# Sliding-window attention times a gated block on one core: seven block products in all four token chunks, and the weight work laid out anew

## The chip, the cores and the metric

One core of a Trainium2 chip runs the kernel. Its engines work beside each other, each in the order of its own instruction stream: TensorE (PE, matmuls; PEld loads the stationary operand), VectorE (DVE), ScalarE (ACT), GpSimd (POOL) and SyncE (SP, which here issues every DMA). The metric is the device time of one execution in microseconds.

## The reference, cut to what matters

```python
x = A_x                                   # (1, 2048, 576) float32
xn = layernorm(x)
q, k, v = split(xn @ wqkv)                # 32 heads of 18
p = softmax(mask(q @ k.T * 18 ** -0.5))   # causal, a window of 256 keys
s = (p @ v) @ wo
h = (xn @ w_gate) * (xn @ w_up)           # 4608 features, no nonlinearity
g = silu(h @ w_down)
out = x + s * g
```

All inputs are float32. The kernel reaches that accuracy with 16-bit floats by splitting each operand into a high and a low half and adding three products (high x high, high x low, low x high). The gate and up products and the down product are most of the matmul work.

## The kernel before, in words

A first stretch normalises x into `XT` (features on partitions, 2048 tokens along the row, high and low halves), makes v, then q and k, and stores them to DRAM. It is over about 179 us into the profiled execution. Then the main part runs in 72 slots: 18 groups of 256 features (`g`), and in each group four chunks of 512 tokens (`c`). A slot has 16 places. At each place the program writes out a few gate and up matmuls (`seven_place`, L1075, or in the main loop, L1216) and then everything that `at(slot, place, f, ...)` has put there, with the score matmuls first, then the down products, then the rest in the order in which it was registered. Place numbers beyond 15 run on into the next slots. This list alone sets the order of each engine's stream; the engines then wait for each other where data or buffers ask for it. Four kinds of work share the slots:

- **Gate and up.** In chunks 0, 1 and 2 (`SEVEN`), the product of the group's weights (two blocks of features) and the chunk (two halves of tokens), each also cut in two along the contraction, is made from seven block products in place of eight. They need sums of blocks of the input (`SX`, `XD` and parts of `XT` overwritten, made once by `s_steps`, whose places and engines are in `SUMS_AT` and `SUMS_ON`) and sums of blocks of the weights (`TF` and, split into halves, `TW`, made for each group by `t_sum` on POOL, `t_hi` on ACT, `t_lo` on DVE). A slot has 100 such matmuls of 256 columns. Products are added up in PSUM or by reading a bank (`seven_read`): product 0 is copied by ACT (L1043), and product 1 is then added on in the same bank; five others go through DVE (L1047); four multiplications of gate by up follow, three on POOL and one on DVE (L1053). In chunk 3 the slot has 52 full matmuls of 512 columns and four half ones, one ACT copy (L924) and one DVE multiplication (L929) for each of two feature tiles.
- **Down.** `down` (eight times a slot, at places 7 to 21 of the next slot, six matmuls each, L952) multiplies the result by the group's down weight into a single bank `dn`, and DVE adds each to the accumulator (L957) before the next can start. `h_hi` (L934, ACT) and `h_lo` (L939, DVE) split the input of it.
- **Attention.** Step `s` stands in slot `s + 1`: loads of k, q and v, scores (L826), maximum on DVE (L834), exponent on ACT (L840, L844, L847), the low half of the probabilities (`turn_probs`, L855, on POOL or DVE), a transposing DMA (L858), the product with v (`weigh`, L867), `finish` and, every fourth step, stores (`store_o`).
- **The next group's weights.** `ffn_raw` loads them (each gate and up load in two pieces of two DMAs, L147 and L149; the down weight, L373), `ffn_amax` takes maxima (L380, DVE), `ffn_spread_out` and `ffn_spread_in` send them through DRAM to all partitions, `ffn_scale` makes scales (L400, then L127 to L131), `up_hi`, `dn_hi` and `t_hi` are ACT's high halves (L152), `up_lo`, `dn_lo` and `t_lo` DVE's low halves (L155), and `dn_low` a scaled copy on POOL (L525). For group `g` they are placed relative to slot 4g - 4, most of them in places 38 to 68.

At the end the output weight is prepared the same way (`wo_*`), and `o_out` makes 16 output tiles (L1178, L1181).

Of the kernel before, what the change touches and what calls it, by code (L numbers as in the profile page):

```python
# [20 lines left out]
def kernel(  # L21
# [71 lines left out]
    def up_ring():  # L93
        return ring.tile([128, 10, 128], F16, name="upw", bufs=8)
# [174 lines left out]
    def square(dst, src):  # L269
        nc.scalar.activation(junk[0:src.shape[0], 0:src.shape[-1]], src, AF.Square, accum_out=dst)  # L270
# [41 lines left out]
    def qk_split(m):  # L312
        if m < QM:
            w = UW["q", m] = up_ring() if m < 8 else pro.tile([128, 10, 128], F16, name="wq8")
# [67 lines left out]

    def ffn_spread_out(g):
# [34 lines left out]
    SEVEN = (0, 1, 2)  # L418
    TF, TW, SX, XD = {}, {}, {}, {}

    def seven(sl):
        return sl % NCH in SEVEN

    def t_sum(g, kind, pair, i):
        r = RAW[g, kind].rearrange("p k (f n) -> p k f n", f=2)
        b = {(k, f): r[:, 2 * k:2 * k + 2, f] for k in range(2) for f in range(2)}
        if i == 0:
            TF[g, kind, pair] = sums.tile([128, 2, 2, 128], F32, name="tf", bufs=2)
        t = TF[g, kind, pair]
        if pair == 0:  # L430
            x0, x1 = (b[0, 1], b[0, 0]) if i == 0 else (b[1, 1], t[:, 0])
        else:
            x0, x1 = (b[1, 0], TF[g, kind, 0][:, 1]) if i == 0 else (b[1, 1], b[0, 1])
        nc.gpsimd.tensor_tensor(t[:, i], x0, x1, op=OP.subtract)

    def t_hi(g, kind, pair):
        if pair == 0:
            TW[g, kind] = sums.tile([128, 4, 2, 2, 128], F16, name="tw", bufs=2)
        w = TW[g, kind][:, 2 * pair:2 * pair + 2, 0]
        hi(w, TF[g, kind, pair], SC[g][:, 6 + kind:7 + kind])  # L440

    def t_lo(g, kind, pair):
        w = TW[g, kind][:, 2 * pair:2 * pair + 2]
        lo(w[:, :, 1], TF[g, kind, pair], SC[g][:, 6 + kind:7 + kind], w[:, :, 0])
# [5 lines left out]
    def s_steps(c):  # L450
# [13 lines left out]
        def do(e, to, x, y, f):  # L464
            if to in ("w", "z") and to not in t:
                t[to] = sums.tile([128, 2, 2, 128], F32, name="tf", bufs=2).rearrange("p a b n -> p a (b n)")
# [86 lines left out]
    SUMS_AT = ((-24, -24, -24, -23, -22, -22, -22, -17, -16, -16, -15, -15, -14, -13, -12, -11, -11),  # L553
               (-22, -22, -22, -20, -19, -18, -18, -18, -17, -17, -14, -14, -13, -12, -12, -12, -7),
               (-10, -10, -9, -8, -6, -5, -4, 3, 4, 5, 6, 7, 8, 9, 10, 11, 13))
    SUMS_ON = ("vvvvppvpvvpppvvvp", "ppppvpvpvvppvpvpv", "ppvvvpvpvvvpvpvpv")
    for c in SEVEN:
# [5 lines left out]
    for n in range(4):  # L563
        at(0, (-9, -9, -7, -7)[n], t_sum, 0, 0, n // 2, n % 2)
        at(0, (-3, -2, -1, -1)[n], t_sum, 0, 1, n // 2, n % 2)
    for n in range(4):
        at(0, (-4, -4, 0, 0)[n], t_hi, 0, n // 2, n % 2)
        at(0, (-3, -2, 1, 1)[n], t_lo, 0, n // 2, n % 2)
# [120 lines left out]
    for t in range(16):  # L689
# [35 lines left out]
        for m in range(QM):  # L725
            for c in (2 * half, 2 * half + 1):
# [4 lines left out]
                if half == 1:  # L731
                    if m in (1, 2, 3):
                        ffn_amax(0, m - 1, c - 2)
                    if m >= QM - 2:
                        k = 2 * (m - QM + 2) + c - 2
                        up_hi(0, k)
                        up_lo(0, k)
# [29 lines left out]
            else:  # L767
                if m == 3:
                    ffn_spread_out(0)
                if m == 5:  # L770
                    ffn_spread_in(0)
                if m == 6:
                    ffn_scale(0)
# [76 lines left out]
    PL_AT = ((), (0, 1, 2, 3))  # L850

# [407 lines left out]
```

## Time and profile before

| | |
|---|---|
| time, median of 3 runs | 1617.65 us (1616.84 to 1618.41) |
| the profiled execution | 1621.29 us, its span 1619.6 us |
| clock granted to PE, mean | 0.999 |
| PE busy | 1586.2 us, 98% of the span |
| DVE busy | 1307.6 us, 81% |
| ACT busy | 1115.0 us, 69% |
| POOL busy | 818.3 us, 51% |
| instructions | 39383 |

The profile is that of one execution. Times of single rows count from the start of its span. A row of the timeline has start, length, engine, line, operation, output and inputs, shapes and a count; in brackets stands the idle time of the engine before it and what ended it. A row of the windows view gives for one stretch the busy time of each engine with its number of instructions, the granted clock, the share of the DMA engines' time and the rate. A row of the groups gives the shapes and the count, then busy us and the mean ns of one, then the idle time before them. A row of the waits gives the total us, how often, and the longest.

### The profile page before, as it was taken

The numbers are of one execution on the slowest core, as the hardware profiler recorded it, in microseconds if no ns is written. First come the engines' busy times: TensorE is split into PE (matmuls) and PEld (weight loads), VectorE is DVE, ScalarE is ACT, GpSimd is POOL, SyncE is SP. The second block draws the span as 40 slices with busy tenths as digits, with TensorE's granted clock in tenths as the row PEclk, the third lists the DMA queues.
The fourth block names the chain that finished last, engine by engine and source line by source line (L and its number), as shares of the span: only waits on it lengthen the run. The fifth ranks groups of instructions, "written<-read, shape, count | busy, mean of one in ns | idle before, by whom it ended". The sixth has DMA issues, their size and how long they took to land.

```text
span 1619.6 us, 39383 instructions
## 1 busy us (share of the span) xinstructions
PE 1586.2 (98%) x14706; PEld 1164.2 (72%) x14706; DVE 1307.6 (81%) x3120; ACT 1115.0 (69%) x2180; POOL 818.3 (51%) x1050
## 2 busy tenths in 40 slices
PE   8999899999999999999999999999999999999999
PEld 5464577786868676768686777777786868686777
DVE  7536788888887989798989888888988898977644
ACT  6433487778787878787878778887878787843230
POOL 3114464556455656566665657465656565633100
PEclk9999999999999999999999999999999999999999
DMA  9572446565758786978787887878677879760158
GB/s 231 176 187 87 129 76 128 87 129 95 127 103 132 132 135 126 136 135 131 132 138 138 128 146 112 155 113 150 118 149 118 155 115 154 121 129 1 23 115 217
DMA packets 548768, 206.83 MB, mean 128 GB/s; under 512 B 489376, under 2 KB 529376, under 8 KB 548576
## 3 DMA queue, kind: packets, MB, share of 16 engines
q1 hardware_dynamic: 548576, 204.31, 67.5%
q8 instruction: 115, 1.88, 0.5%
q14 instruction: 77, 0.63, 0.1%
HBM read 76.63 MB, written 23.75 MB: 62 GB/s over the span
## 4 chain that ended last, share of the span: by engine, by line
PE 79%; DVE 12%; DMA 5%; issue 2%; POOL 1%; ACT 1%; SPq 0%; DVEq 0%; POOLq 0%; ACTq 0%
PE up L1075 27%; PE dn L952 21%; PE up L1216 10%; PE pv L867 3%; PE s L342 3%; DVE acc L957 2%; PE s L826 2%; DVE upw L155 2%; PE s L952 2%; PE s L1178 2%; PE up L1178 1%; DMA sd_f<-both 1%; PE up L342 1%; DVE gt L1047 1%; DVE ht L1053 1%
## 5 line engine op out<-in xcount | busy, mean ns | idle before, releaser
L952 PE MATMUL dn<-dnw,hh 128*128 128x288 f16 x3168 | 477.5, 286 | 14.4 <-DVE acc L957 13.2
L952 PEld LDWEIGHTS <-hh 128*128 128x128 f16 x3456 | 328.6, 98 | 150.7 <-issue 55.3
L957 DVE SCALAR_TENSOR_TENSOR acc<-dn,sc,acc 128x288 f32<-128x288 f32 x496 | 254.6, 513 | 136.0 <-PE dn L952 130.4
L840 ACT ACTIVATE mx<-mx,sig 128x1 f32<-128x1 f32 x512 | 195.3, 384 | 182.0 <-DVE mx L834 173.3
L1075 PEld LDWEIGHTS <-upw 128*128 128x128 f16 x2592 | 242.1, 97 | 33.1 <-issue 1.3
L1075 PEld LDWEIGHTS <-tw 128*128 128x128 f16 x2592 | 238.8, 97 | 32.9 <-issue 3.6
L1075 PE MATMUL up<-XT,upw 128*128 128x256 f16 x1728 | 253.9, 272 | 0.7 <-ACT gt L1043 0.7
L1216 PE MATMUL up<-XT,upw 128*128 128x512 f16 x936 | 232.0, 378 | 0.0
L1047 DVE SCALAR_TENSOR_TENSOR gt<-up,gt 128x512 f32<-128x512 f32 x270 | 184.7, 684 | 20.0 <-PE up L1075 16.5
L1053 POOL TENSOR_TENSOR ht<-gt 128x256 f32<-128x256 f32 x162 | 125.5, 788 | 125.8 <-ACT gt L1043 111.6
L1075 PE MATMUL up<-sx,tw 128*128 128x256 f16 x1296 | 175.6, 273 | 4.0 <-ACT gt L1043 2.2
L1075 PE MATMUL up<-XT,tw 128*128 128x256 f16 x1296 | 168.1, 273 | 0.0
L867 PEld LDWEIGHTS <-pt 128*128 128x128 f16 x2880 | 137.6, 96 | 29.0 <-DMA pt<-pp 1.8
L867 PE MATMUL pv<-vt,pt 128*128 128x37 f16 x2880 | 143.0, 179 | 0.6 <-DMA pt<-pp 0.6
L1216 PEld LDWEIGHTS <-upw 128*128 128x128 f16 x936 | 82.9, 97 | 68.9
L934 ACT ACTIVATE hh<-ht 128x512 f16<-128x512 f32 x144 | 89.6, 622 | 55.0 <-POOL ht L1053 34.3
L886 POOL CAST ob<-o 128x144 f16<-128x144 f32 x64 | 19.5, 304 | 202.0 <-DVE o L882 202.0
L939 DVE SCALAR_TENSOR_TENSOR hh<-hh,ht 128x512 f16<-128x512 f16 x144 | 110.6, 768 | 0.0
L1043 ACT ACTIVATE gt<-up 128x512 f32<-128x512 f32 x108 | 63.5, 588 | 59.3 <-PE up L1075 58.2
L1075 PE MATMUL up<-sx,upw 128*128 128x256 f16 x648 | 88.2, 273 | 2.4 <-DVE gt L1047 2.4
L380 DVE TENSOR_REDUCE am<-raw 128x1 f32<-128x640 f32 (+1 forms) x108 | 84.0, 790 | 0.0
L155 DVE SCALAR_TENSOR_TENSOR upw<-raw,sc,upw 128x640 f16<-128x640 f32 x72 | 76.7, 1065 | 0.3 <-ACT upw L152 0.3
(2289 smaller groups left out, 2967.4 us busy)
## 6 DMA issues: line engine op xcount, KB each, us to landing
raw<-in_B_w_down_dram SPq DMA_DIRECT2D x36, 288.0 KB
qk_d<-qp SPq DMA_DIRECT2D x18, 512.0 KB
raw<-in_B_w_gate_dram SPq DMA_DIRECT2D x36, 256.0 KB
raw<-in_B_w_up_dram SPq DMA_DIRECT2D x36, 256.0 KB
vt<-v_d SPq DMA_DIRECT2D x48, 111.0 KB
ks<-qk_d SPq DMA_DIRECT2D x96, 54.0 KB
v_d<-vo SPq DMA_DIRECT2D x16, 296.0 KB
xr<-in_A_x_dram SPq DMA_DIRECT2D x16, 288.0 KB
```

The source lines that it names most:

```text
L155: nc.vector.scalar_tensor_tensor(w, rv, s, h, op0=OP.mult, op1=OP.subtract)
L380: nc.vector.tensor_reduce(SC[g, "am"][:, half, kind:kind + 1], r, axis=AX.X if kind == 2 else AX.XY, op=OP.max, apply_absolute_value=True)
L840: nc.scalar.activation(mx[:, 1:2], mx[:, 0:1], AF.Identity, bias=sig[:, 2:3], scale=sig[:, 1:2])
L867: nc.tensor.matmul(PVB[s][:, j, i, :VW], pt[:, 2 * nb * j + n], VT[s][:, lo_ + n % nb, j * VW:(j + 1) * VW], start=n == 0, stop=n == 2 * n ...
L934: nc.scalar.activation(hh[:, 0], h, AF.Copy, scale=1.0 / LO)
L939: nc.vector.scalar_tensor_tensor(hh[:, 1], hh[:, 0], -LO, h, op0=OP.mult, op1=OP.add)
L952: nc.tensor.matmul(ps[:, :HALF], a, b, start=q == 0, stop=q == len(l) - 1)
L957: nc.vector.scalar_tensor_tensor(d, ps[:, :HALF], SC[g][:, 9:10], d, op0=OP.mult, op1=OP.add)
L1047: nc.vector.scalar_tensor_tensor(seven_new(sl, name), CH[q], H_SC, x, op0=OP.mult, op1=OP.add)
L1053: eng.tensor_tensor(HT[sl, f][:, 256 * i:256 * i + 256], u[:, 0:256], u[:, 256:512], op=OP.mult)
L1075: nc.tensor.matmul(CH[q][:, o], a, b, start=CH["first"], stop=last and q != 4, skip_group_check=q in ON)
L1216: nc.tensor.matmul(banks[up], a, b, start=i == 0 and not up, stop=i == 12 and up == 1)
```

## The change

All four chunks use the seven products; the code of the full products is gone. Around that:

- `s_steps` runs for chunk 3 too, and the places and engines of all sums are new, nearly all of them ahead of slot 0. Scratch for some of them is cut from the tile `rqk`.
- Group 0's weights are split ahead of slot 0; its bound comes from sums of squares on ACT (`first_bound`) for gate and up.
- For the other groups every piece of the weight work has a new place, from place 6 of the group before's first slot to place 5 of its own first slot. Block sums live in four tiles of two blocks (`TW[g, kind, pair]`); one sum of each kind is made twice, so POOL makes ten for each group, and not eight.
- The ring of split gate and up weights has six buffers, not eight.
- All low halves of the probabilities are made on POOL.
- The attention output tile holds two steps, not four, and is stored twice as often; the output weight's steps move; the last part writes its result in place of the accumulator and has no `yt`.

```diff
     def up_ring():
-        return ring.tile([128, 10, 128], F16, name="upw", bufs=8)
+        return ring.tile([128, 10, 128], F16, name="upw", bufs=6)
...
+    def first_bound(kind):
...
+            square(am[:, 0, kind:kind + 1], RAW[0, kind].rearrange("p k n -> p (k n)"),
+                   rv.rearrange("p k n -> p (k n)").bitcast(BF))
...
-    SEVEN = (0, 1, 2)
...
+    def t_sum(g, kind, n):
...
+        T0, T1, T3, T2 = (2, 1, 0, 3) if g == 0 else (0, 1, 0, 1)
+        to, x0, x1 = ((T0, b[0, 1], b[0, 0]), (T1, b[1, 1], t[:, T0]), (T3, b[1, 1], b[0, 1]),
+                      (T2, b[1, 0], t[:, T1]), (T0, b[0, 1], b[0, 0]))[n]
+        nc.gpsimd.tensor_tensor(t[:, to], x0, x1, op=OP.subtract)
...
-            TW[g, kind] = sums.tile([128, 4, 2, 2, 128], F16, name="tw", bufs=2)
...
+        w = TW[g, kind, pair] = sums.tile([128, 2, 2, 2, 128], F16, name="tw", bufs=4)
...
-    for c in SEVEN:
+    SUMS_AT = ((-26, -26, -26, -25, -24, -24, -23, -23, -22, -22, -21, -21, -20, -20, -20, -19, -18),
+               (-26, -26, -25, -25, -24, -24, -23, -22, -22, -21, -20, -20, -20, -20, -19, -19, -18),
+               (-17, -17, -16, -16, -15, -15, -14, -12, -11, -10, -9, -9, -8, -7, -6, -5, -1),
+               (-12, -11, -11, -10, -9, -8, -8, -7, -6, -6, -5, -4, -3, -3, -2, -1, 1))
+    SUMS_ON = ("v" * 17, "p" * 17, "v" * 7 + "p" * 10, "p" * 17)
+    for c in range(NCH):
...
+    for k in range(4):
+        at(0, -7 + k, up_hi, 0, k)
+        at(0, -6 + k, up_lo, 0, k)
...
-        (nc.gpsimd if j or i in PL_AT[seven(s + 1)] else nc.vector).tensor_tensor(pp[:, a + n:a + 2 * n], sm, pp[:, a:a + n], op=OP.subtract)
+        nc.gpsimd.tensor_tensor(pp[:, a + n:a + 2 * n], sm, pp[:, a:a + n], op=OP.subtract)
...
-                    at(b, ((0, 1, 2, 6, 10, 14) if g == 1 else (-6, -2, 2, 6, 10, 14))[2 * kind + part],
-                       ffn_raw, g, kind, part)
-                for half in range(2):
-                    at(b, ((9, 13) if g == 1 else (9, 9), (14, 26), (24, 29))[kind][half], ffn_amax, g, kind, half)
-            at(b, 30, ffn_spread_out, g)
-            at(b, 34, ffn_spread_in, g)
-            at(b, 40, ffn_scale, g)
-            for k, (ph, pl) in enumerate(((43, 45), (44, 47), (49, 53), (55, 57))):
...
-                at(b, (38, 39, 42, 44)[n], t_sum, g, 0, n // 2, n % 2)
-                at(b, (50, 51, 54, 55)[n], t_sum, g, 1, n // 2, n % 2)
...
-                at(b, (47, 47, 52, 57)[n], t_hi, g, n // 2, n % 2)
-                at(b, (48, 49, 56, 58)[n], t_lo, g, n // 2, n % 2)
-        for k, (ph, pw, pl) in enumerate(((57, 62, 64), (64, 68, 65)) if g else ((64, 65, 66), (68, 69, 70))):
...
+            at(b, (45, 47)[k] if g else 64 + k, dn_hi, g, k)
+            at(b, (46, 49)[k] if g else 65 + k, dn_lo, g, k)
+            at(b, (49, 51)[k] if g else 66 + k, dn_low, g, k)
...
+                at(b, (6, 9, 12, 15, 18, 21)[2 * kind + part], ffn_raw, g, kind, part)
+            for half in range(2):
+                at(b, (14, 16, 20, 22, 25, 27)[2 * kind + half], ffn_amax, g, kind, half)
+        at(b, 28, ffn_spread_out, g)
+        at(b, 32, ffn_spread_in, g)
+        at(b, 38, ffn_scale, g)
+        for k in range(4):
+            at(b, (40, 42, 62, 64)[k], up_hi, g, k)
+            at(b, (41, 44, 63, 65)[k], up_lo, g, k)
+        for kind in range(2):
+            for n in range(5):
+                at(b, ((40, 41, 43, 60, 61), (44, 46, 48, 61, 62))[kind][n], t_sum, g, kind, n)
+            for pair in range(2):
+                at(b, ((57, 58), (64, 66))[pair][kind], t_hi, g, kind, pair)
+                at(b, ((58, 59), (67, 69))[pair][kind], t_lo, g, kind, pair)
...
-        at(NSLOT - 4, 2 * k, wo_raw, k)
-        at(NSLOT - 4, 2 * k + 6, wo_amax, k)
-        at(NSLOT - 2, 3 * k, wo_split, k)
-    at(NSLOT - 3, 0, wo_out)
-    at(NSLOT - 3, 6, wo_in)
-    at(NSLOT - 3, 9, wo_scale)
+        at(NSLOT - 4, 2 * k + 6, wo_raw, k)
+        at(NSLOT - 4, 2 * k + 14, wo_amax, k)
+        at(NSLOT - 2, 3 * k + 2, wo_split, k)
+    at(NSLOT - 3, 8, wo_out)
+    at(NSLOT - 3, 12, wo_in)
+    at(NSLOT - 2, 0, wo_scale)
```

More of the change, by code (lines that the diff above doesn't have):

```diff
@@ new lines @@
+        if g == 0:
+            continue
+        for kind in range(3):
+            for part in range(2):
+                at(b, (6, 9, 12, 15, 18, 21)[2 * kind + part], ffn_raw, g, kind, part)
+            for half in range(2):
+                at(b, (14, 16, 20, 22, 25, 27)[2 * kind + half], ffn_amax, g, kind, half)
[5 more added lines that the diff above has]
+            at(b, (41, 44, 63, 65)[k], up_lo, g, k)
@@ L998, in seven_unit @@
         for kind in range(2):
[L999 removed]
+            w1, w2 = UW[g, kind], UW.get((g, 2 + kind))
             w, k = {0: (w1, 0), 1: (w1, 2), 6: (w2, 2)}.get(q, (None, 0))
[L1001 to L1002 removed]
+            if w is not None:
+                wh, wl = w[:, k:k + 2], w[:, 5 + k:7 + k]
+            else:
+                pair, n = {2: (0, 1), 3: (0, 0), 4: (1, 0), 5: (1, 1)}[q]
+                wh, wl = (TW[g, kind, pair][:, n, i] for i in range(2))
             if q in (2, 4, 6):
```

191 lines of the change are left out of this document (79 added, 112 removed).

## The prediction

> **What bounds the kernel now.** I read the page first, then the busy time slot by slot, then the waits at the places that the change touches.
>
> ```profile
> PE 1586.2 (98%) x14706; PEld 1164.2 (72%) x14706; DVE 1307.6 (81%) x3120; ACT 1115.0 (69%) x2180; POOL 818.3 (51%) x1050
> ```
> ```profile
> core 0: us, PE busy (x) PEld busy (x) DVE busy (x) ACT busy (x) POOL busy (x), PEclk, DMA share, GB/s
> 712.88:731.75 18.87, 18.87 (x206) 15.54 (x204) 17.25 (x42) 14.28 (x29) 12.16 (x14) 1.00 0.93 174
> 731.75:750.62 18.87, 18.87 (x206) 15.54 (x204) 15.35 (x41) 14.08 (x29) 10.08 (x14) 1.00 0.76 132
> 750.62:769.52 18.90, 18.90 (x206) 15.56 (x204) 15.26 (x42) 15.53 (x31) 12.73 (x20) 1.00 0.95 128
> 769.52:790.24 20.72, 20.01 (x163) 11.23 (x160) 20.25 (x45) 19.12 (x37) 11.77 (x14) 1.00 0.63 105
> 178.89:196.82 17.93, 13.16 (x103) 9.82 (x101) 14.14 (x21) 6.37 (x11) 14.43 (x15) 0.90 0.43 120
> ```
>
> The first four windows are one group: chunks 0, 1, 2 with seven products, chunk 3 with full ones. In the first three PE never rests; they are as short as their matmuls allow. The chunk 3 slot is 1.83 us longer, and there DVE is busy 20.25 of 20.72 us. So the kernel is bound by PE, except in chunk 3, where the weight work crowds DVE and ACT. The last window, slot 0, I use below.
>
> Small slacks keep PE busy in a seven-product slot. The down products (L952) share one bank, so each waits until DVE's addition (L957) has emptied it:
>
> ```profile
> 733.22 0.90 PE L952 MATMUL dn<-dnw,hh 128*128 128x288 f16 x6
> ...
> 754.28 0.27 PE L1075 MATMUL up<-XT,upw 128*128 128x256 f16 x1
> ...
> 760.93 0.90 PE L952 MATMUL dn<-dnw,hh 128*128 128x288 f16 x6
> ...
> 768.79 0.90 PE L952 MATMUL dn<-dnw,hh 128*128 128x288 f16 x6
> ...
> 774.89 0.90 PE L952 MATMUL dn<-dnw,hh 128*128 128x288 f16 x6 [0.71 <-DVE acc L957]
> ```
>
> The last row shows the wait when DVE is late. The row at 754.28 is the first matmul of product 1, which overwrites the bank that ACT must first copy (L1043).
>
> **The change, part by part.**
>
> *Products in chunk 3.* 18 slots go from 20.7 to 18.87 us: 18 x 1.83 = 32.9 us less, matmul time and DVE wait together. The order of PE's instructions bears it out: 44 matmuls more in each of 18 slots. DVE gains five additions and one product there and loses two multiplications and four of the probabilities' subtractions, which go to POOL; all this is what the other three slots bear already.
>
> *Raw weights and their maxima, chunk 0.* The gate weight's second piece is issued at place 9, behind the four loads of q, and its maximum stands on DVE at place 14. Before, a down weight piece was issued just there (place 10), and another maximum stood at place 14:
>
> ```profile
> 724.03 0.41 SPq L147 DMA_DIRECT2D raw<-in_B_w_up_dram  x1
> 724.49 0.54 SPq L149 DMA_DIRECT2D raw<-in_B_w_up_dram  x1
> ...
> 727.18 2.32 SPq L806 DMA_DIRECT2D qs<-qk_d  x4
> 729.54 0.42 SPq L373 DMA_DIRECT2D raw<-in_B_w_down_dram  x1
> ...
> 885.94 0.42 SPq L373 DMA_DIRECT2D raw<-in_B_w_down_dram  x1
> ```
> ```profile
> 730.64 0.81 DVE L380 TENSOR_REDUCE am<-raw 128x1 f32<-128x640 f32 x1
> 731.37 0.68 DVE L1047 SCALAR_TENSOR_TENSOR gt<-up,gt 128x512 f32<-128x512 f32 x1
> 731.97 0.51 DVE L957 SCALAR_TENSOR_TENSOR acc<-dn,sc,acc 128x288 f32<-128x288 f32 x1
> ```
> ```profile
> 602.03 3.42 DMA tf<-sd_f
> ```
>
> SP reaches the place at 729.54 (16.66 us into the slot; in the slot that begins at 867.57, 18.37 in). A piece is two DMAs, so the second goes out at 730.0. The nearest landing I have is the 192 KB read, 3.42 us after its issue: 733.4. DVE is there at 730.64 and waits 2.8 us. Behind it in the queue are 0.73 us of maximum, the 0.60 of L1047 and L957's 0.51: done at 735.2, where PE's next down product was due at 733.22. PE loses 2.0 us, or 3.7 where SP is as late as at 885.94; nothing if the landing took 1.4 us. I take 2.3, in 15 groups (those whose loads meet attention's): **+34.5**. The other pieces go out five to eight places ahead of their maxima and, by the same lag of SP, land about when DVE comes: 0.
>
> *The scale, chunk 2.* It moves from place 8 to place 6, ahead of the addition that frees the bank for 760.93:
>
> ```profile
> 760.26 0.52 DVE L957 SCALAR_TENSOR_TENSOR acc<-dn,sc,acc 128x288 f32<-128x288 f32 x1 [0.82 <-PE dn L952]
> ...
> 761.76 0.69 DVE L400 TENSOR_REDUCE sc<-tf 128x3 f32<-128x384 f32 x1
> ...
> 763.18 0.51 DVE L957 SCALAR_TENSOR_TENSOR acc<-dn,sc,acc 128x288 f32<-128x288 f32 x1
> ```
>
> The five instructions take 1.42 us (761.76 to 763.18). The gap before 760.26 holds 0.82, so the addition ends at 761.3, 0.4 after PE wants it. The two DMAs before the scale are issued two places earlier as well, so their lateness stays. 0 to 1.3; I take 0.5 x 16 = **+8**.
>
> *From chunk 2 to 3, and from 3 to 0.* At a slot's end ACT has no gap between the scores and the copy of product 0:
>
> ```profile
> 747.65 0.86 ACT L840 ACTIVATE mx<-mx,sig 128x1 f32<-128x1 f32 x2 [1.81 <-DVE mx L834]
> ...
> 752.89 0.58 ACT L1043 ACTIVATE gt<-up 128x512 f32<-128x512 f32 x1
> ...
> 764.19 0.51 ACT L847 CAST pp<-sm__12089 128x384 f16<-128x384 f32 x1
> 764.61 1.55 ACT L152 ACTIVATE upw<-raw,sc 128x640 f16<-128x640 f32 x2
> ...
> 783.13 0.71 ACT L152 ACTIVATE tw<-tf,sc 128x512 f16<-128x512 f32 x1
> 783.74 0.76 ACT L152 ACTIVATE dnw<-raw,sc 128x576 f16<-128x576 f32 x1
> ```
>
> From 747.65 on it works through to 753.47, and PE needs the copy at 754.28: slack 0.81. The change puts two down-weight casts (2 x 0.67, overlap taken off) into this run in chunk 2, so the copy is 0.53 late; the low half of an up weight (1.07, row below) now stands at place 12, ahead of the addition for 768.79, which had 0.77 to spare, in the same stretch. Together 0.5 to 1.3, taken as 0.6 x 16 = **+9.6**.
>
> At the end of chunk 3 the run gets two up-weight casts and one of the sums: 2 x 0.75 + 0.63 = 2.1, so 1.3 late. There is more: the sums' casts at places 9 and 10 stand before and behind a pair of probabilities that in chunk 2 ended at 764.70, so the second is done about 765.9. DVE's low half waits for it, and behind that are the reductions that end attention's step and the next scores:
>
> ```profile
> 765.11 0.20 DVE L878 RECIPROCAL rc<-pv 128x8 f32<-128x8 f32 x1
> ...
> 767.51 0.51 DVE L957 SCALAR_TENSOR_TENSOR acc<-dn,sc,acc 128x288 f32<-128x288 f32 x1
> 768.41 1.48 DVE L155 SCALAR_TENSOR_TENSOR upw<-raw,sc,upw 128x640 f16<-128x640 f32 x1
> ```
> ```profile
> L155 DVE SCALAR_TENSOR_TENSOR upw<-raw,sc,upw 128x640 f16<-128x640 f32 x72 | 76.7, 1065 | 0.3 <-ACT upw L152 0.3
> ```
>
> They start at 766.6 in the place of 765.11. The addition that ended at 768.02 ends near 769.5, 0.7 after PE wants it, and ACT's run starts later too. So 1.3 to 2.7; I take 1.8 x 16 = **+28.8**. The row at 768.41 shows what POOL's sums next to DVE add: 1.48 us for one low half of an up weight, against a mean of 1.07. The Trainium skill ("SBUF — State Buffer", section "SBUF: two separate sides") says that DVE reading two SBUF inputs and POOL reading SBUF exclude each other for a whole instruction; the row agrees, and the rule speaks for the upper end of these terms.
>
> *POOL in chunk 3.* The 10.1 us of chunk 1, five of the ten block sums (eight before) and the two 1/2048 copies:
>
> ```profile
> L525 POOL TENSOR_SCALAR dnw<-dnw 128x576 f16<-128x576 f16 x36 | 67.8, 1882 | 7.9 <-ACT dnw L152 7.9
> L434 POOL TENSOR_TENSOR tf<-raw,tf 128x256 f32<-128x256 f32 x72 | 59.7, 829 | 11.3 <-ACT qp L333 8.3
> ```
>
> 10.1 + 5 x 0.83 + 2 x 1.88 = 18.0 of 18.87. The copies stand before a subtraction whose transposed result is needed seven places later; 0 here, since PE's late start above covers it, else up to 1 us a group.
>
> *Before slot 0, the end, the rest.* Group 0's splits and most sums move ahead of slot 0.
>
> ```profile
> PE up L1075 <- DVE gt L1047: 3.0, 3, 1.7
> PE up L1075 <- ACT gt L1043: 2.9, 2, 2.2
> ```
>
> These sum to 5.9; the longest of the first row (1.7) is the wait for the output weight's scale near the end, the other 4.2 lie in slot 0. I take **-4**; the 17 added steps of chunk 3 could give back as much before slot 0. The output weight's maximum and its scale come one place closer: **+1**. Half-size output tiles mean 32 more DMAs on SP, hidden by its waits for probabilities; six weight buffers suffice, since two are free when the next pair is written and the other two are read last at place 13. Results written in place: nothing.
>
> *Sum.* -32.9 + 34.5 + 8 + 9.6 + 28.8 - 4 + 1 = +45. The profiled execution took 1621.29 us (span 1619.6), 3.6 over the median: 1666 there, 1663 as a median.
>
> **Rivals.** *Faster: the seven-product slot keeps its shape.* If DVE's wait for the gate piece and ACT's late copy don't occur, only the first and last terms stand: 1617.65 - 32.9 - 3 = 1582. For it speaks the load: a group's DVE work, 68.1 us in the four windows, is 90% of 4 x 18.87, and the chunk 0 window has 91% without a wait. Against it: the waits come from order, not load. It decides at (32.9 + 3)/16 = 2.2 us of waits a group; above that the kernel is slower.
>
> *Slower still: the clock.* After waits in slot 0 the clock fell:
>
> ```profile
> 189.17 2.20 PE L1075 MATMUL up<-sx,tw 128*128 128x256 f16 x12 [2.21 <-ACT gt L1043]
> ...
> 752.97 1.47 PE L1075 MATMUL up<-sx,tw 128*128 128x256 f16 x12
> ```
>
> The same twelve matmuls took 2.20 after an idle 2.21 us, and the window has a clock of 0.90. A whole slot like it is 13.16 us busy for 10.7 of work (98 matmuls at the second row's step, (1.47 - 0.27)/11 = 0.109): 2.5 us. Once a group in 15 groups this gives 1663 + 37 = 1700. The Trainium skill ("TensorE: Matmul & The Clock Gate", Part 1) lets the clock fall only after an idle window of about 3.4 us; by that rule waits of 2 to 3 us leave it whole and 1663 stands. The row differs from the rule, so the case keeps a chance.
>
> **How the numbers follow.** Forecast 0.58 (own range 1636 to 1690: its 81 us of waits a third smaller or larger); slower still 0.14; faster 0.25; no change 0.03. A measurement tells about 0.2% (3 us) from nothing. The faster cases spread from 1582 to 1614, and I leave out about half; at the top I take in the clock case and the upper ends of the waits: 1592 to 1712. Slower 0.72, same 0.03, faster 0.25.
>
> **What would show it.** Chunk 0 slots near 21 us with DVE's maximum waiting for a raw weight's DMA over 2 us; product 1 of chunks 3 and 0 waiting for ACT's copy; the down product after the scale waiting for DVE; a group of about 80.6 us against the 77.4 of the four windows. I am wrong if groups last 76 us, or if the DMA lands before DVE comes; and the size is off if PE's clock falls below 1.00 in chunk 0.

## The result, and the profile after

The changed kernel took 1771.42 us (median of 4 runs, 1766.80 to 1777.38), the kernel before, on the same chip, 1618.01 us (1616.84 to 1618.41). The ratio is 1.095, interval 1.0915 to 1.0988: slower. Its profiled execution took 1768.96 us, the span is 1767.2 us against 1619.6, and the mean clock granted to PE 0.984 against 0.999.

The first line of the page of the changed kernel answers to the first line of the prediction:

```profile
PE 1609.7 (91%) x15498; PEld 1248.3 (71%) x15498; DVE 1354.2 (77%) x3131; ACT 1118.1 (63%) x2190; POOL 979.8 (55%) x1214
```

PE is busy 23.5 us longer, but its share falls from 98% to 91%: most of the 147.6 us is PE at rest. The windows view of the changed kernel shows where: the stretch before slot 0, then slots 44 to 47, one group, chunk by chunk.

```profile
core 0: us, PE busy (x) PEld busy (x) DVE busy (x) ACT busy (x) POOL busy (x), PEclk, DMA share, GB/s
98.40:198.01 99.61, 86.37 (x478) 46.91 (x476) 58.38 (x86) 35.94 (x70) 50.01 (x50) 0.91 0.35 102
1118.01:1138.70 20.69, 19.21 (x206) 15.47 (x204) 17.32 (x40) 16.66 (x33) 15.21 (x18) 1.00 0.76 132
1138.70:1162.30 23.60, 20.80 (x206) 16.31 (x204) 17.94 (x44) 13.65 (x28) 9.39 (x13) 0.93 0.66 141
1162.30:1185.97 23.67, 20.75 (x206) 16.06 (x204) 17.04 (x44) 17.02 (x34) 14.87 (x21) 0.93 0.66 106
1185.97:1205.86 19.89, 19.19 (x206) 15.53 (x204) 16.77 (x41) 15.04 (x31) 16.02 (x18) 1.00 0.51 91
```

The first row's stretch in the kernel before:

```profile
98.40:178.89 80.49, 80.49 (x479) 45.24 (x477) 45.65 (x75) 28.94 (x56) 28.77 (x32) 1.00 0.42 126
```

So slot 0 begins 19.1 us later: PE rests for 13.2 us of the longer stretch, and for the other 5.9 it is busy longer with the same matmuls, at a clock of 0.91. The group lasts 87.9 us against the 77.4 of the prediction's four windows. All four slots have rest of PE in them, and in chunks 1 and 2 PE is also busy 1.6 us longer than in chunks 0 and 3, for the same matmuls, at a clock of 0.93. DVE is never busy for more than 17.94 us of a slot: no engine is full over a whole slot.

I cut both traces at the first gate or up matmul of each slot. The table gives the mean of 15 slots for each chunk (slots 4 to 63) and, behind the stroke, how much of that PE rested; "start" is when slot 0 begins, "end" is slots 64 to 71 and what follows.

| us | start | slot 0 | slots 1 to 3 | chunk 0 | chunk 1 | chunk 2 | chunk 3 | end |
|---|---|---|---|---|---|---|---|---|
| before | 178.9 | 17.9 | 54.9 | 18.76 / 0.00 | 18.82 / 0.04 | 18.96 / 0.16 | 20.66 / 0.74 | 209.7 |
| after | 198.0 | 12.7 | 53.8 | 21.12 / 1.92 | 22.69 / 2.98 | 22.10 / 2.57 | 20.06 / 0.88 | 213.1 |
| difference, all slots | +19.1 | -5.2 | -1.1 | +35.4 | +58.0 | +47.1 | -9.0 | +3.4 |

Chunk 3, which has the fewer products now, gives back 9 us; the three chunks whose matmuls are the same cost 140. The waits of PE in the group shown are these (timeline of the changed kernel, PE and DVE rows in order of time):

```profile
1122.90 0.27 PE L1084 MATMUL up<-XT,upw 128*128 128x256 f16 x1 [1.07 <-ACT gt L1052]
...
1140.35 0.82 DVE L381 TENSOR_REDUCE am<-raw 128x1 f32<-128x640 f32 x1 [2.68 <-DMA raw<-in_B_w_gate_dram]
1142.24 1.57 PE L959 MATMUL dn<-dnw,hh 128*128 128x288 f16 x6 [1.92 <-DVE acc L964]
1143.84 2.38 PE L1084 MATMUL up<-sx,tw 128*128 128x256 f16 x12
...
1157.87 0.75 DVE L381 TENSOR_REDUCE am<-raw 128x1 f32<-128x576 f32 x1 [0.94 <-DMA raw<-in_B_w_down_dram]
1161.57 0.90 PE L959 MATMUL dn<-dnw,hh 128*128 128x288 f16 x6 [0.88 <-DVE acc L964]
1173.11 0.66 DVE L413 TENSOR_REDUCE sc<-tf 128x3 f32<-128x384 f32 x1 [2.00 <-DMA tf<-sd_f]
1175.06 0.90 PE L959 MATMUL dn<-dnw,hh 128*128 128x288 f16 x6 [2.29 <-DVE acc L964]
```

Three times DVE stands before a DMA that has not landed (a gate piece, a down piece, the maxima sent through DRAM), and each time the addition queued behind it frees the down bank late. The waits view of the changed kernel has the totals, and one row of the kernel before for comparison:

```profile
PE dn L959 <- DVE acc L964: 90.8, 82, 2.9
DVE am L381 <- DMA raw<-in_B_w_gate_dram: 42.5, 16, 3.5
DVE sc L413 <- DMA tf<-sd_f: 25.4, 15, 2.6
PE up L1084 <- ACT gt L1052: 24.8, 16, 1.8
DVE am L381 <- DMA raw<-in_B_w_down_dram: 14.9, 13, 2.2
```
```profile
PE dn L952 <- DVE acc L957: 13.2, 18, 1.0
```

Ahead of slot 0 the first block sum on DVE (at place -26; before it stood at -24) waits 15.74 us for the DMA that transposes the last piece of x, with v's additions queued behind it, and PE waits for those. The third wait is for a copy that SP issues only at 149.28, behind the stores of v:

```profile
116.14 0.69 DVE L487 TENSOR_TENSOR sx<-XT 128x512 f32<-128x512 f16 x1 [15.74 <-DMA XT<-xh]
120.37 5.97 PE L294 MATMUL s<-wv,XT 128*128 128x288 f16 x28 [8.10 <-DVE vo L304]
...
153.48 1.01 PE L351 MATMUL s<-XT,upw 64*128 64x512 f16 x3 [3.89 <-DMA XT<-XT]
```

In the kernel before the same sum waits for the same DMA and starts at about the same time, but v's additions up to 105.77 stand ahead of it, and PE never rests in this stretch:

```profile
115.34 0.69 DVE L468 TENSOR_TENSOR sx<-XT 128x512 f32<-128x512 f16 x1 [8.75 <-DMA XT<-xh]
```

That sum reads tokens of chunk 0, not of the last piece. Its tile lies in the memory pool that the kernel opens when it closes the one with the transposes' source `xh`, so it probably waits for that memory to be free; this is read off the kernel, and no run tests it.

### The profile page after: what moved, and what is told of

It reads as the page before. It is cut to its first block, busy times and chain, and to the rows that moved or that the text cites. A ratio compares the mean times of both kernels' runs of the same rounds, so it can differ in the third digit from the quotient of the medians.

```text
span 1767.2 us, 41080 instructions
## 1 busy us (share of the span) xinstructions
PE 1609.7 (91%) x15498; PEld 1248.3 (71%) x15498; DVE 1354.2 (77%) x3131; ACT 1118.1 (63%) x2190; POOL 979.8 (55%) x1214
## 3 DMA queue, kind: packets, MB, share of 16 engines
q8 instruction: 121, 1.98, 0.5%
## 4 chain that ended last, share of the span: by engine, by line
PE 35%; DVE 21%; DMA 12%; ACT 10%; SPq 9%; issue 6%; POOL 6%; ACTq 0%; POOLq 0%; DVEq 0%
PE up L1084 13%; PE dn L959 9%; DMA tf<-sd_f 4%; SPq L875 3%; DVE acc L964 3%; DMA raw<-in_B_w_down_dram 3%; DVE gt L1056 3%; DMA raw<-in_B_w_gate_dram 3%; POOL pp L872 3%; ACT pp L866 3%; PE s L343 3%; SPq L818 2%; SPq L825 2%; PE s L959 2%; DVE tw L155 2%
## 5 line engine op out<-in xcount | busy, mean ns | idle before, releaser
L1084 PE MATMUL up<-XT,upw 128*128 128x256 f16 x2304 | 340.6, 273 | 24.8 <-ACT gt L1052 24.8
L1084 PEld LDWEIGHTS <-tw 128*128 128x128 f16 x3456 | 322.0, 98 | 46.0 <-issue 6.2
L1056 DVE SCALAR_TENSOR_TENSOR gt<-up,gt 128x512 f32<-128x512 f32 x360 | 246.2, 684 | 57.8 <-PE up L1040 35.6
L1062 POOL TENSOR_TENSOR ht<-gt 128x256 f32<-128x256 f32 x216 | 178.3, 832 | 161.9 <-ACT gt L1052 123.0
L1084 PE MATMUL up<-sx,tw 128*128 128x256 f16 x1728 | 241.3, 278 | 0.1
L1084 PE MATMUL up<-XT,tw 128*128 128x256 f16 x1728 | 224.6, 273 | 5.4 <-DVE gt L1056 5.4
L1052 ACT ACTIVATE gt<-up 128x512 f32<-128x512 f32 x144 | 84.3, 585 | 72.9 <-PE up L1084 72.9
L381 DVE TENSOR_REDUCE am<-raw 128x1 f32<-128x640 f32 (+1 forms) x104 | 82.4, 792 | 58.6 <-DMA raw<-in_B_w_gate_dram 42.5
L1084 PE MATMUL up<-sx,upw 128*128 128x256 f16 x864 | 117.7, 273 | 0.0
L155 DVE SCALAR_TENSOR_TENSOR upw<-raw,sc,upw 128x640 f16<-128x640 f32 x72 | 80.3, 1115 | 17.9 <-ACT upw L152 17.8
L447 POOL TENSOR_TENSOR tf<-raw 128x256 f32<-128x256 f32 x102 | 88.2, 865 | 0.1
L155 DVE SCALAR_TENSOR_TENSOR tw<-tf,sc,tw 128x512 f16<-128x512 f32 x68 | 59.8, 880 | 21.5 <-ACT tw L152 21.5
```

The source lines that it names most:

```text
L155: nc.vector.scalar_tensor_tensor(w, rv, s, h, op0=OP.mult, op1=OP.subtract)
L447: nc.gpsimd.tensor_tensor(t[:, to], x0, x1, op=OP.subtract)
L1052: nc.scalar.activation(seven_new(sl, name), CH[q], AF.Copy, scale=H_SC)
L1056: nc.vector.scalar_tensor_tensor(seven_new(sl, name), CH[q], H_SC, x, op0=OP.mult, op1=OP.add)
L1062: eng.tensor_tensor(HT[sl, f][:, 256 * i:256 * i + 256], u[:, 0:256], u[:, 256:512], op=OP.mult)
L1084: nc.tensor.matmul(CH[q][:, o], a, b, start=CH["first"], stop=last and q != 4, skip_group_check=q in ON)
```

## The experiments

The theory after this reading (A): the loss is waits of PE that come from the order of work on DVE and ACT, and matmuls that the clock slows after the longest of them. The rival (B): DVE, ACT and POOL have too much to do in a slot of 18.9 us, so a wait taken away comes back elsewhere. Unless a line says otherwise, nothing is left out of a kernel's computation. Times are of one execution each (the four of the changed kernel lie 10.6 us apart), beside the kernel before on the same chip (1620.4 for the first four, 1624.1 for the next two, 1618.7 for e7 and e8, 1621.0 for the last four). The means by chunk of all of them:

| | time | start | slot 0 | chunk 0 | chunk 1 | chunk 2 | chunk 3 |
|---|---|---|---|---|---|---|---|
| e1_raw | 1726.85 | 197.2 | 12.7 | 21.30 | 19.31 | 22.44 | 20.17 |
| e2_sums | 1783.85 | 187.8 | 19.5 | 20.98 | 23.40 | 22.62 | 20.21 |
| e3_scale | 1783.09 | 196.4 | 12.7 | 21.23 | 24.36 | 21.18 | 20.17 |
| e4_three | 1705.49 | 188.0 | 19.7 | 21.18 | 19.37 | 20.95 | 20.30 |
| e5_slow3 | 1657.44 | 177.9 | 17.9 | 18.76 | 20.83 | 18.99 | 20.65 |
| e6_slow4 | 1685.91 | 178.2 | 17.9 | 18.74 | 22.56 | 18.96 | 20.65 |
| e7_spread | 1664.3 | 189.8 | 17.3 | 20.75 | 18.82 | 19.44 | 20.16 |
| e8_late | 1666.41 | 182.6 | 14.5 | 20.75 | 18.98 | 19.44 | 20.13 |
| e9_bare | 1603.71 | 197.8 | 12.7 | 18.88 | 18.75 | 18.77 | 18.78 |
| e10_bare_before | 1600.76 | 178.0 | 17.9 | 18.74 | 18.75 | 18.77 | 19.73 |
| e11_casts | 1685.40 | 197.3 | 12.7 | 21.14 | 18.75 | 20.56 | 19.98 |
| e12_shift | 1661.59 | 186.7 | 20.7 | 20.87 | 18.83 | 19.53 | 19.73 |

### The raw weights loaded earlier

```diff
-                at(b, (6, 9, 12, 15, 18, 21)[2 * kind + part], ffn_raw, g, kind, part)
+                at(b, ((6, 9, 12, 15, 18, 21) if g == 1 else (0, 2, 4, 6, -10, -6))[2 * kind + part], ffn_raw, g, kind, part)
```

> The changed kernel with nothing altered but the places of the raw weight loads (down weight at -10 and -6, gate at 0 and 2, up at 4 and 6; group 1 as it was). Theory A (a piece lands after DVE has come to its maximum, and everything behind it on DVE is late): both waits of the chunk 1 slots go, their mean falls from 22.7 to about 19.2 us, the kernel from 1771 to about 1720. Theory B (DVE and ACT have simply too much to do, the DMA wait only shows it): the wait moves to the next instructions, less than 15 us are gained.

It took 1726.85 us, 42 less than the changed kernel. Chunk 1 fell from 22.69 to 19.31 us (51 us in 15 slots), the others were 0.1 to 0.3 us longer. So DVE's waits for raw weights and what follows from them cost 42 to 51 us.

### The block sums of chunks 0 and 1 two places later

```diff
-    SUMS_AT = ((-26, -26, -26, -25, -24, -24, -23, -23, -22, -22, -21, -21, -20, -20, -20, -19, -18),
-               (-26, -26, -25, -25, -24, -24, -23, -22, -22, -21, -20, -20, -20, -20, -19, -19, -18),
+    SUMS_AT = ((-24, -24, -24, -23, -22, -22, -21, -21, -20, -20, -19, -19, -18, -18, -18, -17, -16),
+               (-24, -24, -23, -23, -22, -22, -21, -20, -20, -19, -18, -18, -18, -18, -17, -17, -16),
```

> The changed kernel with the block sums of chunks 0 and 1 two places later (from -24 in place of -26), nothing else. If DVE's wait of 15.7 us at the first sum holds up the evictions of v, PE's waits of 8.1 and 3.9 us before slot 0 go and slot 0 begins near 180 us in place of 198: 1771 to about 1753. If the 17 steps added for chunk 3 are what fills the stretch, slot 0 still begins after 193.

A miss. Slot 0 began 10.2 us sooner, a little over half of the 18 expected, but lasted 6.8 us longer: PE waits there 4.36 us for ACT's copy of product 0, which stands behind the last sums and group 0's casts. Of the gain at the start 3.4 us are left. The total is above the changed kernel's, since chunk 1, which the edit does not touch, came out at 23.40 us: how long PE rests behind the gate weight's maximum differs from group to group (1.35 to 2.74 us in the changed kernel's trace) and from run to run, so only the stretch before slot 1 is to be read here.

### The scale two places later

```diff
-        at(b, 38, ffn_scale, g)
+        at(b, 40, ffn_scale, g)
```

> The changed kernel with the scale at place 40 in place of 38, nothing else. Theory A (order): the wait of the down product after the scale (about 1.9 us, with the clock's fall behind it) goes, chunk 2 slots fall from 22.1 to about 20.3, the kernel by about 25 us to 1746. Theory B (load): DVE is as late two places on, less than 8 us.

Also a miss. The wait behind the scale at the middle of chunk 2 is gone, but another of 1.98 us stands near the slot's end, and chunk 2 fell by 0.92 us only. (Chunk 1, not touched, is 1.7 us longer again, and the clock is below 0.97 in 22 of the 60 slots, where the changed kernel has 11; the total says nothing here.) e4_three, below, has the same row, with DVE's part around it (timeline of e4_three):

```profile
1128.78 0.68 DVE L413 TENSOR_REDUCE sc<-tf 128x3 f32<-128x384 f32 x1
...
1131.18 0.91 DVE L155 SCALAR_TENSOR_TENSOR upw<-raw,sc,upw 128x640 f16<-128x640 f32 x1 [0.47 <-ACT upw L152]
...
1135.28 1.58 DVE L155 SCALAR_TENSOR_TENSOR upw<-raw,sc,upw 128x640 f16<-128x640 f32 x1
...
1137.94 0.90 PE L959 MATMUL dn<-dnw,hh 128*128 128x288 f16 x6 [1.97 <-DVE acc L964]
1138.28 1.15 DVE L155 SCALAR_TENSOR_TENSOR dnw<-raw,sc,dnw 128x576 f16<-128x576 f32 x1
```

The scale now waits for nothing, but everything that needs it follows in one stretch: the scale's instructions, two up low halves (the same instruction takes 0.91 and 1.58 us) and a down low half in ten us. Here B is right for chunk 2: DVE has the time over the slot, not over these places.

### The three edits together

> All three of these edits together. Theory A: the gains add up or more, since waits under 2 us leave the clock whole: 1771 - 51 - 18 - 25 = about 1677, with the clock about 1660 and its mean back above 0.995; what remains above 1582 is ACT's late copy in chunk 0 and the waits between chunks 2 and 3. Theory B: above 1730.

1705.49 us, clock 0.990: between the two expectations. The gains of the loads stay, chunk 2 keeps its 1.97 us wait, chunk 0 its 1.63 us wait for ACT's copy. The expectation had waits under 2 us leave the clock whole; that did not hold, for the clock falls six times in the 60 slots, each time behind a rest of 1.77 to 1.97 us.

### Waits of a known length in the kernel before

To see what a wait itself costs, a maximum that DVE has just taken is taken three or four times more, with the same result, at place 14 of each group's first slot in the kernel before.

```diff
+            for _ in range(4):
+                at(b, 14, ffn_slow, g)
```

> The kernel before with three more maxima on DVE (0.8 us each, of data that is there, results unchanged) at place 14 of each chunk 0 slot, where the changed kernel's DVE waits for the raw weight. DVE's slack there is 0.6 us, so PE waits about 1.8 us in 16 slots: 1618 + 29 = 1647, and the clock stays at 1.00 in the chunk 1 slots if only waits above 2 us bring it down.

> The same with four: PE waits about 2.6 us in 16 slots. If a wait costs its own length alone: 1618 + 42 = 1660. If a wait above 2 us also brings the clock down for some microseconds (about 1.6 us lost each time): 1685, with a clock near 0.93 in the chunk 1 slots.

The chunk 1 slot of one group (windows view, then the PE timeline; e5_slow3 with three):

```profile
1066.96:1087.70 20.74, 19.03 (x207) 15.54 (x204) 17.67 (x44) 14.23 (x29) 10.06 (x14) 1.00 0.75 134
```
```profile
1070.29 0.90 PE L956 MATMUL dn<-dnw,hh 128*128 128x288 f16 x6 [1.71 <-DVE acc L961]
1071.18 1.47 PE L1081 MATMUL up<-sx,tw 128*128 128x256 f16 x12
```

And e6_slow4 with four:

```profile
1082.76:1105.93 23.17, 20.60 (x206) 16.27 (x204) 18.49 (x45) 14.22 (x29) 10.04 (x14) 0.93 0.63 118
```
```profile
1086.95 1.08 PE L956 MATMUL dn<-dnw,hh 128*128 128x288 f16 x6 [2.57 <-DVE acc L961]
1088.06 2.73 PE L1081 MATMUL up<-sx,tw 128*128 128x256 f16 x12
```

The wait is 0.86 us longer, the slot 2.43 us: PE is busy 1.57 us longer for the same work, the twelve matmuls take 2.73 us and not 1.47, and the clock of the slot is 0.93. That is the picture of chunks 1 and 2 of the changed kernel. That slower matmuls follow a long wait is shown here with nothing else changed. They do not follow every one: of e6's sixteen such waits behind slot 4, 2.40 to 2.72 us long, eleven were followed by them, and five were not (those slots last 21.2 to 21.6 us at a clock of 1.00). In e5 one of the sixteen was 2.04 us long, and it alone had the slower clock behind it. Against the kernel before, e5 took 33 us more (29 expected) and e6 62 us more, between the 42 of the waits alone and the 67 of the waits with the clock; eleven falls of the clock are in keeping with that.

### Without the weight work

e9_bare is the changed kernel and e10_bare_before the kernel before, each without any weight work of groups 2 on (all 18 groups run, so these are groups 2 to 17, where the expectation says 15); those groups multiply by group 1's weights, so the output is another one.

```diff
-    for g in range(NG):
+    for g in range(2):
...
-            h, w = HT[sl, ft], DW[g, ft]
+            h, w = HT[sl, ft], DW[min(g, 1), ft]
```

> The changed kernel without the weight work of groups 2 to 15: no loads, maxima, scale, casts, low halves and POOL sums of them; these groups multiply by group 1's weights, so the output is another one. What is left is seven products in all chunks and the longer work ahead of slot 0. Theory A (the seventh product fewer is worth what chunk 3's eighth product cost, 20.66 against 18.8 us, and all the loss is the weight work's): all four chunks 18.4 to 18.9 us, chunk 3 included, time 1595 to 1615 us. Rival C (seven products in all four chunks cost something by themselves, in the attention's share of DVE or ACT): chunk 3 or another above 19.5 us, time above 1640 us.

> The kernel before without the weight work of groups 2 to 15 (these groups multiply by group 1's weights, so the output is another one). Theory A: the weight work of the kernel before lies beside TensorE almost whole (its traced waits are about 13 us in all), so 1600 to 1616 us, chunk 3 at 20.5 us or little less. If the weight work costs the kernel before as much as the changed one: below 1590 us.

The first of the four slots 44 to 47 of e9_bare (the others are 18.87, 18.86 and 18.87 us), then the chunk 3 slot of e10_bare_before (windows):

```profile
1015.02:1033.88 18.86, 18.86 (x206) 15.54 (x204) 13.62 (x37) 14.04 (x29) 10.04 (x14) 1.00 0.75 115
```
```profile
1065.35:1085.17 19.82, 19.82 (x162) 11.24 (x160) 13.17 (x37) 14.82 (x30) 5.77 (x8) 1.00 0.59 95
```

1603.71 and 1600.76 us, both inside what A gave; only e10's chunk 3 is shorter than expected. Three things follow. Seven products in all four chunks cost nothing by themselves: of the 60 slots only slot 4, where group 1's last casts still stand, rests. A slot with full products is 19.82 us and not 20.7: of the 1.83 us that chunk 3 was longer, about half (0.95 by the means, 19.73 - 18.78) were its matmuls, the other half was the weight work in that slot, which the change does not remove. And the weight work costs the kernel before 20 us, the changed one 165.

### The casts alone

e11_casts is the changed kernel with all casts, low halves and POOL sums at their places, made each time from group 1's raw weights and scale; the loads, maxima, exchange and scale of later groups are left out, so the output is another one.

```diff
-        for kind in range(3):
+        if g == 1:
+            for kind in range(3):
...
-        hi(w[:, 0:5], RAW[g, k % 2][:, :, k // 2 * 128:k // 2 * 128 + 128], SC[g][:, 6 + k % 2:7 + k % 2])
+        hi(w[:, 0:5], RAW[min(g, 1), k % 2][:, :, k // 2 * 128:k // 2 * 128 + 128], SC[min(g, 1)][:, 6 + k % 2:7 + k % 2])
```

> The changed kernel with the casts, low halves and POOL sums of every group at their places, but from group 1's raw weights and scale: the loads, maxima, exchange of the maxima and scale of groups 2 to 15 are left out, so the output is another one. Theory A (loads and maxima cost chunk 1, the scale part of chunk 2, the casts chunk 0's copy and the rest of chunk 2): chunk 1 at 18.4 to 19.2 us instead of 22.7, chunk 0 still at 20.8 to 21.2 with the 1.6 us wait for ACT's copy, chunk 2 at 19.5 to 21, time 1670 to 1695 us. Rival (the casts' load on DVE and ACT is the whole loss): above 1730 us.

1685.40 us. Chunks 0 to 2 of one group (windows):

```profile
1064.64:1085.88 21.24, 19.20 (x206) 15.46 (x204) 17.89 (x41) 17.19 (x34) 15.76 (x19) 1.00 0.61 107
1085.88:1104.75 18.87, 18.87 (x207) 15.54 (x205) 13.63 (x37) 14.06 (x29) 10.06 (x14) 1.00 0.64 105
1104.75:1125.71 20.96, 19.17 (x206) 15.51 (x204) 16.34 (x39) 16.27 (x33) 13.45 (x17) 1.00 0.77 111
```

As theory A said: chunk 1 is as short as e9's, chunk 0 as long as the changed kernel's, chunk 2 lies between. Taken away in this order, the casts make 82 of the 165 us of weight work (1603.71 to 1685.40); the loads, maxima, exchange and scale make 84 (1685.40 to 1768.96). The clock is 1.00 in these slots, where no wait is over 1.8 us; of the 60 slots one is below (slot 12, 0.92, behind a wait of 1.77 us).

### Other places for the casts

e7_spread is e4 with the casts at places where ACT and DVE rest in e4's trace, and the up loads six places later; e12_shift moves more casts, and puts the down weight's loads and maxima ahead of those of gate and up; e8_late is e7 with chunk 3's block sums after slot 0 and the others at the places of the kernel before. The cut below is e7_spread against the changed kernel.

```diff
-            at(b, (45, 47)[k] if g else 64 + k, dn_hi, g, k)
+            at(b, (44, 52)[k] if g else 64 + k, dn_hi, g, k)
...
-            at(b, (40, 42, 62, 64)[k], up_hi, g, k)
+            at(b, (40, 44, 62, 70)[k], up_hi, g, k)
...
-                at(b, ((57, 58), (64, 66))[pair][kind], t_hi, g, kind, pair)
+                at(b, ((57, 58), (68, 68))[pair][kind], t_hi, g, kind, pair)
```

> On top of the three edits of e4, every cast and low half of a group's weights is put where ScalarE and VectorE stand idle in e4's trace: the second up pair's casts behind the copy of product 0, the down casts apart from the up casts, no two low halves in one place. Nothing is left out. Theory A (the loss is the waits of PE for ACT's copy, 1.63 us a group, and for DVE's eviction, 1.97 us a group, and the slower matmuls that follow the long one): chunk 0 falls from 21.2 to about 19.3 us a slot, chunk 2 from 20.95 to about 19.2, chunk 3 from 20.3 to about 19.7; the time about 1640 us with a clock of 0.997 or more. Theory B (ACT and DVE are so full, 93% of a seven-product slot on DVE, that a wait taken away at one place comes back at another): above 1690 us, with the waits at other places.

> As e7, and the block sums of chunks 0 to 2 at the places that the kernel before has for them, those of chunk 3 (17 steps) in slots 0 and 1 instead of ahead of slot 0. Nothing is left out. If the work of the block sums ahead of slot 0 (17 steps more, a POOL step about 1.2 us) is what made the start of slot 0 later: slot 0 begins near 180 us instead of 188 and ends near 198 instead of 207.7, the time 9 to 12 us under e7's, slots 1 to 3 at most 2 us longer. If the start is set by something else, or the steps only move into slots 1 to 3, where DVE is 91% busy: within 4 us of e7.

> e7 with the second up pair's two casts both behind the copy of product 0, the raw loads and maxima of gate and up later and those of the down weights first, and the down weights' low halves at places 54 and 57. Nothing is left out. Theory A (a wait whose cover is made does not come back): the copy's 0.70 us wait in chunk 0 goes, chunk 0 from 20.75 to about 19.7 us, chunk 3 from 20.2 to about 19.7, chunk 1 at 19, time about 1640 us. Theory B (DVE is 91 to 96% busy in these slots, so what is taken from one place is paid at another): within 8 us of e7's 1664 or above it, with waits for DVE at places that had none.

e7 took 1664.3 us, 41 under e4, 24 over what A gave. Its slots of chunks 0 and 3 in one group (chunks 1 and 2 are 18.88 and 19.54 us), and waits of PE in them:

```profile
1049.58:1070.41 20.83, 19.42 (x206) 15.56 (x204) 18.88 (x42) 17.18 (x34) 14.83 (x19) 1.00 0.85 157
...
1108.83:1129.16 20.33, 19.18 (x207) 15.51 (x204) 19.61 (x42) 15.86 (x32) 17.91 (x19) 1.00 0.65 110
```
```profile
1054.11 0.27 PE L1084 MATMUL up<-XT,upw 128*128 128x256 f16 x1 [0.70 <-ACT gt L1052]
1062.86 0.61 PE L1084 MATMUL up<-sx,tw 128*128 128x256 f16 x4 [0.53 <-DVE tw L155]
...
1108.09 0.90 PE L959 MATMUL dn<-dnw,hh 128*128 128x288 f16 x6 [0.48 <-DVE acc L964]
```

The long waits are gone (the copy's 1.63 is 0.70, chunk 2's 1.97 is 0.48) and the clock with them is 1.00. But short ones are left, and one, at product 4 for a low half that e4 had in time, is new: both theories have part of it. DVE is now busy for 18.88 and 19.61 us in chunks 0 and 3.

e12_shift took 1661.59. Chunk 3 is a little shorter (19.73), chunk 0 is not: the 0.70 us wait for the copy is still there though no weight cast stands before it any more. ACT's split of the hidden values, ahead of the copy, now waits for a multiplication on POOL, which is busy for 17.77 us of the chunk 3 slot before (timeline of e12_shift, POOL, ACT and PE):

```profile
1049.77 0.72 POOL L1062 TENSOR_TENSOR ht<-gt 128x256 f32<-128x256 f32 x1
1050.53 0.63 ACT L941 ACTIVATE hh<-ht 128x512 f16<-128x512 f32 x1 [0.82 <-POOL ht L1062]
1051.07 0.58 ACT L1052 ACTIVATE gt<-up 128x512 f32<-128x512 f32 x1
1051.69 0.27 PE L1084 MATMUL up<-XT,upw 128*128 128x256 f16 x1 [0.70 <-ACT gt L1052]
```

By its number on record that is theory B's case. The reading that fits e7 and e12 is this: with the long waits gone, three engines are each nearly full in some slot, and a wait taken from one is paid at the next. It rests on two layouts; that no better one exists is not shown.

e8_late: slot 0 ended at 197.1 us, where the kernel before has it (196.8), but slots 1 to 3 took 63.6 us and not 53.3, and the time is 2 us over e7's. The rival's second case came true: chunk 3's 17 sum steps cost about ten us on either side of slot 0.

No kernel here that does all the work is faster than the one before. The bound for the change as it stands is e9_bare's 1604 us; with this weight work the best was 1662.

## Why the prediction was right or wrong

The sign and the main places were right, the size was not: +45 us was forecast, +147.6 came (span against span), above the range's end of 1712. Of the 103 us between the two, about 30 lie in chunk 2 (its two terms, 17.6, became 47.1), 23 in chunk 1 (34.5 became 58), 18 in chunk 3, 19 ahead of slot 4 (each slot of chunk 3 counted with a gain of 1.83 where it stands), and 13 in chunk 0 and at the end. By its steps:

- **Products in chunk 3 (-32.9).** This step failed: 15 of its 18 slots are in the table, for which it gave -27.5; they gave -9.0, 18 us less. The prediction took 20.7 - 18.87 as "matmul time and DVE wait together" and let both go. e10_bare_before shows that the matmuls are 0.95 us of it, 14 us in 15 slots. The other half was weight work, which in the changed kernel still costs chunk 3 1.3 us a slot (20.06 against 18.78) and is counted on top in the other chunks.
- **Raw weights and maxima (+34.5).** The step for the gate piece held: DVE waited 42.5 us in 16 groups, 2.7 each against the 2.8 forecast, and PE's rest behind it was 1.35 to 2.74 us in the 15 groups, 2.0 in the mean, where 2.3 was taken. "The other pieces ... 0" failed: the down piece made DVE wait 14.9 us more, at the end of chunk 1. With the clock this makes +58 in chunk 1; e11_casts, where chunk 1 is 18.75, shows that all of it hangs on loads and maxima.
- **The scale (+8).** Failed in the words "so their lateness stays". The part of chunk 2 that is not casts is 22.10 - 20.56, 23 us: DVE waited 25.4 us in 15 groups for the maxima's way through DRAM (before: 2.0 us in 3). The two DMAs stand two places earlier, but SP serves its queue in order, and between them now stand two output stores and a transpose that waits for POOL's probabilities (timeline of the changed kernel, SP):

```profile
1162.83 0.81 SPq L137 DMA_DIRECT2D sd_f<-both  x1
...
1164.17 1.72 SPq L913 DMA_DIRECT2D o_d<-ob  x2
1166.00 2.95 SPq L875 DMA_TRANSPOSE pt<-pp  x1
1169.05 0.53 SPq L408 DMA_DIRECT2D tf<-sd_f  x1
```

  The read goes out 6.2 us after the write; in the kernel before, in the same group, it was 3.6, with one store and one transpose between. The half-size output tiles' stores, "hidden by its waits for probabilities" in the prediction, are 1.72 us of this; no run took them away alone. The cure two places later only moved the wait to the low halves (e3_scale).
- **Chunk 2 to 3 (+9.6).** Undersized: the casts cost chunk 2 20.56 - 18.77, 27 us, and chunk 3 another 18 that the prediction didn't have.
- **Chunk 3 to 0 (+28.8).** Held: +35.4 in chunk 0, its rest 1.92 us a slot against the 1.8 forecast, with the copy of product 0 named (24.8 us in the waits). e11_casts has it unchanged without loads, e7_spread halves the wait by moving the casts, though chunk 0 falls by 0.37 us only.
- **POOL in chunk 3 (0, else up to 1 us).** Waits for late transposed probabilities came in four chunk 3 slots (0.53 to 1.42 us); they are inside the chunk 3 term. That POOL is nearly full there, e12_shift shows (17.77 us of a slot of 19.82).
- **Before slot 0 (-4).** Failed with the wrong sign: +13.9. The prediction allowed 4 us back "before slot 0" and looked at slot 0's waits alone. Slot 0 did get shorter by 5.2, but it begins 19.1 later, by the waits and the slower matmuls shown above. e2 has the first block sums two places later and begins 10.2 us sooner, and e2 and e8 show that the sum work can be moved into slots 0 to 3, where it costs 7 to 10 us again.
- **The end (+1).** +3.4.
- **The clock (a rival with 0.14, 1700).** The sum had nothing for it; it was no rival but part of the outcome. Of the 60 slots of the table 11 have a clock below 1.00 in the changed kernel, by 1.7 us of full clock each (0.07 of 23.67 us), 19 us in all; e11_casts has one such slot. Ahead of slot 0 it is the 5.9 us more of busy PE. The 19 us are 1.25 a group, where the rival took 2.5. It should have been added in part as soon as the waits were forecast at two us and over.
- **The faster rival (0.25).** Its argument, 90% of DVE's time against room for all, is not borne out by e7 and e12: spread as well as I could, the weight work still costs 58 us over e9_bare. It decided at 2.2 us of waits a group; 8.4 us came (the four rests of the table).

## What to carry to other kernels

A slot that is longer than its neighbours is not longer by its matmuls alone: take the other work out of it, on the chip or by its waits, before a gain is read from the difference. When work moves between slots that are each just covered, price it by the longest stretch in which the in-order engine has no gap, not by its share of the slot; and price every DMA that the engine waits for with all that is queued behind it. A wait of two us on a matmul engine that is otherwise always busy can cost more than itself: in e6_slow4 1.6 us more, in eleven groups of sixteen.

## What was not expected of the hardware

The clock can fall after a rest of two us, and the length of the rest alone does not decide. In e6_slow4 the same wait was followed by a fall in one group and not in another:

```profile
1084.11:1087.52 3.41, 0.84 (x8) 0.56 (x6) 3.34 (x8) 1.60 (x4) 0.97 (x2) 1.00 1.17 234
1087.52:1090.93 3.41, 3.41 (x23) 2.18 (x22) 1.33 (x4) 1.96 (x4) 0.91 (x1) 0.50 0.73 174
...
1408.37:1411.79 3.42, 2.71 (x29) 2.21 (x28) 3.28 (x7) 3.26 (x8) 2.94 (x5) 1.00 1.08 139
1411.79:1415.20 3.41, 1.56 (x19) 1.34 (x19) 3.23 (x8) 1.60 (x5) 0.47 (x1) 1.00 0.92 201
1415.20:1418.61 3.41, 3.41 (x37) 2.54 (x35) 2.38 (x6) 1.14 (x3) 0.91 (x1) 1.00 0.95 104
```

These windows are laid on a grid that the trace itself gives: in the slots 4 to 63 of e6 each fall lasts 3.41 us at a clock of 0.50, and the ten falls begin 81.92 us apart (596.00, 677.92 and so on to 1333.28), which is 24 times 3.413. In the first pair of rows the rest of 2.57 us lies within one step of the grid, and the next step has half the clock. In the last three the rest of 2.56 us is split into 0.71 and 1.85, and the clock stays. The falls of the other kernels lie on grids of the same step. Counted over the steps of slots 4 to 63 of the changed kernel and e1, e2, e3, e4, e5, e6 and e11, each step with 2.0 us of rest or more was followed by a fall and none with under 1.6; between the two there are both. The down product of e3_scale that took its usual 0.90 us after a rest of 2.07 us fits: that rest is split into 0.55 and 1.52.

The Trainium skill ("TensorE: Matmul & The Clock Gate", Part 1) has a free-running window of about 3.4 us that must be idle for the clock to fall. The free-running window and its length agree with the grid; that the whole window must be idle does not: 2.57 us of rest were enough in the first pair of rows.

DVE's wait for the gate weight was 0.97 to 3.46 us in the groups of the changed kernel's trace, and a DVE maximum placed in front of an addition hands such a delay to PE. Chunk 1 was 22.69, 23.40 and 24.36 us in the changed kernel, e2_sums and e3_scale, which have the same chunk 1; PE rested for 2.98, 3.22 and 3.88 us of it, and 6, 10 and 12 of the 15 slots have a fall of the clock.
